# A planned instruction order: shared PSUM banks, a new price for changes of array use, and a seeded local search

## The chip, the cores and the metric

The kernel runs on one core of a Trainium2 chip. The metric is device time in microseconds (us) of one launch; lower is better. The engines are TensorE (PE, its weight loads are PEld), VectorE (DVE), ScalarE (ACT), GpSimd (POOL) and SyncE (SP), which issues nearly all DMAs. PSUM has eight banks of 512 float32 columns on 128 partitions; TensorE writes its products there, ScalarE and VectorE read them.

## The reference

Three blocks in a row, all in float32:

```python
# attention: q, k, v are (4, 12, 448, 64)
q_n, k_n = rmsnorm(q, g_q), rmsnorm(k, g_k)
attn = softmax(q_n @ k_n.T / 8)
x = (attn @ v), heads joined          # (4, 448, 768)
# gated block: d_ff = 1024
u, v = split(relu(x @ w_in))
v_s = w_spatial @ layernorm(v) + b_spatial
x = (u * v_s) @ w_out
# mixer: 448 -> 256 -> 448 over tokens, 768 -> 1536 -> 768 over channels
u = x + (relu(x.T @ w_tok1) @ w_tok2).T
out = u + relu(u @ w_ch1) @ w_ch2
```

## The kernel before, in words

**The work.** Attention runs over 24 pairs of heads (a slot each, method `slot` of class `Attention`). A slot loads q and k (`raw`), norms them, transposes them (`tp`), and for each of four groups of 112 queries makes the scores (`scores`, tiles `sc`, two banks a group), their negated row maxima (`nm`, VectorE), the exponentials (`e`, ScalarE), and the transposes of these (`turned`, tiles `tp`, copied out to `et`). From the ninth slot on (`HALVED = 8`) the transposes of a group go by halves of 64 and 48 rows into two banks opened together. `values` multiplies by v (tile `av`). Generators for the gated block (`moe`, products `vps`, `ups`, `sps`, `xps`; weights kept in DRAM as `wu_d`, `wo_d` and loaded as `wu`, `wo`) run beside attention for the batches that are done; the mixer follows: over tokens (`h1ps`, `u_ps`), then over channels (`up` with `h2ps`, `down` with `o_ps`), each by seven products in place of eight. Most products are made of three passes over numbers split into a high and a low part (`PASSES`). Copies of products out of PSUM have names of their own: `tg` for ups, `vr` for vps, `xo` for xps.

**The order.** The kernel does not issue its instructions where it names them. Class `Plan` records each as an `Op` with an engine, dependencies, a planned duration and a delay until others see the result (`estimate`, with fixed prices for each kind: on ScalarE 0.833 ns a column of the free size, 51 for an operand in PSUM, and 93 for each of a bias or scale tile and an accumulated output). At the end `issue` makes the order: `place` runs a list schedule on a planned clock, engine by engine. It takes the waiting instruction with the smallest weight (the most urgent), with these exceptions:

- TensorE: `op.parts` says how the array is used: 0 whole, 1 by halves of the rows, 2 by halves of the columns. An instruction with the same use as the last is preferred if its weight is within `NEAR` or `FAR` of the most urgent. A change of use adds `SWITCH` ns to the planned end.
- VectorE and GpSimd do not run at once where both are marked `port`.
- An instruction that opens PSUM tiles needs banks. `Banks` knows three kinds of tile, `sc` (scores, h1ps), `tp` (transposes) and `mm` (av, vps, ups, sps, xps, u_ps); the products of `up` and `down` rotate over the kinds. Each kind has a number of banks of its own in `OWN`. It may take a free bank only if what the other kinds still lack of their own stays free:

```python
spare = len(free_banks) - sum(max(0, n - held[x]) for x, n in Banks.OWN.items() if x != kind)
if spare < len(ks):
    blocked.append(i)
```

A bank comes free, on the planned clock, when its last reader is done; of the free ones the one that came free first is taken, and tiles of one kind open in the order of the program. Eight rounds alternate a forward placement with one backwards through the graph, whose times become the next weights (there the distances in `BACK` stand for the banks). The round with the shortest planned span gives the order in which all engines' instructions, DMAs on SyncE's queue among them, are written out. One line, 426, writes all instructions, so every row of the profile names L426 and the tiles tell the work apart.

The functions that the change touches:

Of the kernel before, what the change touches and what calls it, by code (L numbers as in the profile page):

```python
# [3 lines left out]

# [21 lines left out]
class Part:  # L26


    def __init__(self, tile_, shape, dtype, steps=(), box=None, dims=None):
        self.tile, self.shape, self.dtype, self.steps = tile_, tuple(shape), dtype, steps  # L30


        self.box = tuple((0, n) for n in self.shape) if box is None else box
        self.dims = tuple(range(len(self.shape))) if box is None else dims
# [94 lines left out]
class Banks:  # L129

    OWN = {"sc": 4, "tp": 2, "mm": 2}
    ALL = 8

    def __init__(self, pool):
        self.pool, self.tiles = pool, {kind: [] for kind in self.OWN}

# [11 lines left out]
class Plan:  # L150
# [112 lines left out]
    def hop(a, b):  # L263

        if a.engine == b.engine and not a.dma:
            return OWN[a.engine]
        return a.late + TO[b.engine]

    def place(self, before, after, lag, weight, tiles=None):
# [11 lines left out]
        if tiles is not None:  # L281
            opens, closes, users = tiles
            users = dict(users)
            free_banks = [(0.0, n) for n in range(Banks.ALL)]
            held = dict.fromkeys(Banks.OWN, 0)
            blocked = []
# [4 lines left out]
        while placed < len(ops):  # L291
# [35 lines left out]
            if tiles is not None and i in opens:  # L327
                ks = opens[i]
                kind = ks[0].psum
                spare = len(free_banks) - sum(max(0, n - held[x]) for x, n in Banks.OWN.items() if x != kind)  # L330
                if spare < len(ks):
# [53 lines left out]
    def issue(self, banks, rounds=8):  # L385

        ops = self.ops
        for op, users in self.later:
            op.deps.update(users)
        number = {op: i for i, op in enumerate(ops)}  # L390
        opens, closes, users, turns, rings = {}, {}, {}, [], []
        for kind, ring in banks.tiles.items():
            for n, t in enumerate(ring):
                us = list(dict.fromkeys(t.users))
                opens.setdefault(number[us[0]], []).append(t)
                users[t] = len(us)
                for u in us:
                    closes.setdefault(number[u], []).append(t)
                if n:
                    turns.append((ring[n - 1].users[0], us[0]))  # L400
                if n >= BACK[kind]:
                    rings.extend((u, us[0]) for u in ring[n - BACK[kind]].users)
        prev, succ, lag, _ = self.graph(turns)
        rprev, rsucc, _, back = self.graph(rings)
        weight = list(range(len(ops)))
        best = None
        for _ in range(rounds):
            start, span, bank = self.place(prev, succ, lag, weight, (opens, closes, users))
            if best is None or span < best[0]:
                best = (span, start, bank)  # L410
            late = [-(start[i] + op.cost) for i, op in enumerate(ops)]
            start, _, _ = self.place(rsucc, rprev, back, late)
            weight = [-(start[i] + op.cost) for i, op in enumerate(ops)]
        start = best[1]
        for t, n in best[2].items():
            t.bank = n
        for i in sorted(range(len(ops)), key=lambda i: (start[i], i)):
            op = ops[i]
            if op.engine == "fence":
                op.call()  # L420
                continue
            for x in (op, *op.more):
                fn, args, kwargs = x.call
                args = [a.real() if isinstance(a, Part) else a for a in args]
                kwargs = {k: a.real() if isinstance(a, Part) else a for k, a in kwargs.items()}
                getattr(getattr(self.nc, op.engine), fn)(*args, **kwargs)  # L426
# [3 lines left out]

SWITCH, NEAR, FAR, EARLY = 200, 2500, 10000, 95000
SHARED = {"vector": "gpsimd", "gpsimd": "vector"}


# [1 line left out]

OWN = {"tensor": 0, "scalar": 143, "vector": 127, "gpsimd": 100, "fence": 0}
TO = {"tensor": 100, "scalar": 0, "vector": 0, "gpsimd": 28, "sync": 0, "fence": 0}  # L440
# [1146 lines left out]
```

## Time and profile before

| | us |
|---|---|
| median of 3 runs | 865.27 |
| lowest, highest | 864.09, 868.58 |
| profiled execution, its own time | 869.1 |
| its span, first to last instruction | 867.3 |
| TensorE busy | 844.7 (97%) |
| VectorE busy | 687.4 (79%) |
| ScalarE busy | 532.5 (61%) |
| GpSimd busy | 416.0 (48%) |

The span is what the profiler sees between the program's first and last instruction; the time of a run also holds what lies around it. Matmuls are pipelined and their ends are modelled, so a share of 97% says that TensorE always had one under way, not that it ran at its best pace. For that one reads the starts of neighbouring pieces.

### The profile page before, as it was taken

Reading aid. Unit: us, or ns where it says so; the run is one execution under the profiler, and the core shown is the slowest. Engines: PE = TensorE matmul, PEld = TensorE weight load, DVE = VectorE, ACT = ScalarE, POOL = GpSimd, SP = SyncE. Lnnn points to the kernel's source line nnn. Section 1 sums busy time; section 2 is a strip of 40 time slices with the busy share of each in tenths; the row PEclk is TensorE's granted clock in tenths of the full one; section 3 lists DMA queues with packets and bytes.
Section 4 is the critical chain, followed back from the end, with each engine's and each line's share of the span. In section 5 each row is a group of like instructions: output and inputs, shape, how many; then the busy total and the mean of one; then the engine's idle time right before and its main releaser. Section 6 shows DMA issues by size and latency. Waiting matters only on the chain.

```text
span 867.3 us, 16458 instructions
## 1 busy us (share of the span) xinstructions
PE 844.7 (97%) x5544; PEld 707.0 (82%) x5544; DVE 687.4 (79%) x1343; ACT 532.5 (61%) x1278; POOL 416.0 (48%) x538
## 2 busy tenths in 40 slices
PE   6999999999999999999899999999999999999998
PEld 4544667777677787777789999999999999999998
DVE  5898899777887678876377577889989886999973
ACT  6999979778787768866253356655435654343331
POOL 3656646785676645566035223234433108425560
PEclk9999999999999999999999999999999999999999
DMA  6555765657636576453778678775765645751441
GB/s 167 148 145 160 193 193 149 199 131 240 185 94 155 144 224 189 107 156 94 245 253 246 209 227 265 246 247 187 206 165 144 204 126 171 237 155 56 146 155 65
DMA packets 153012, 152.34 MB, mean 176 GB/s; under 512 B 76896, under 2 KB 136096, under 8 KB 152928
## 3 DMA queue, kind: packets, MB, share of 16 engines
q1 hardware_dynamic: 152464, 151.26, 59.1%
q8 instruction: 44, 0.72, 0.3%
q14 instruction: 40, 0.33, 0.1%
q10 hardware_dynamic: 464, 0.03, 0.0%
HBM read 112.44 MB, written 38.80 MB: 174 GB/s over the span
## 4 chain that ended last, share of the span: by engine, by line
PE 74%; ACT 8%; DVE 6%; DMA 5%; POOL 3%; issue 2%; SPq 2%; ACTq 0%; POOLq 0%; DVEq 0%
PE h2ps L426 18%; PE o_ps L426 18%; PE xps L426 5%; PE ups L426 5%; PE tp L426 5%; PE av L426 5%; PE vps L426 4%; PE u_ps L426 4%; PE h1ps L426 4%; PE sps L426 3%; PE sc L426 3%; DMA wo<-wo_d 2%; ACT e L426 2%; SPq L426 2%; DMA raw<-in_k_dram 2%
## 5 line engine op out<-in xcount | busy, mean ns | idle before, releaser
L426 PE MATMUL h2ps<-op,w 128*128 128x448 f32 x756 | 154.2, 366 | 0.0
L426 PE MATMUL o_ps<-w,op 128*128 128x384 f32 x882 | 153.1, 334 | 0.0
L426 PEld LDWEIGHTS o_ps<-w,op 128*128 128x128 f32 x882 | 152.9, 188 | 0.0
L426 PEld LDWEIGHTS h2ps<-op,w 128*128 128x128 f32 x756 | 141.7, 188 | 11.1
L426 ACT ACTIVATE e<-sc,nm 112x448 f32<-112x448 f32 x184 | 118.6, 661 | 10.8 <-DVE nm L426 10.4
L426 DVE TENSOR_REDUCE nm<-sc 112x1 f32<-112x448 f32 x192 | 110.2, 613 | 11.3 <-PE sc L426 10.6
L426 POOL TENSOR_TENSOR src<-src 128x384 f32<-128x384 f32 x48 | 64.3, 1348 | 76.8 <-DMA src<-c_d 45.9
L426 ACT ACTIVATE op<-c 128x768 fp32r<-128x768 f32 x49 | 41.5, 847 | 80.6 <-PE o_ps L426 74.8
L426 POOL TENSOR_SCALAR e<-e,sums 112x448 f32<-112x448 f32 x112 | 72.3, 661 | 36.2 <-DVE sums L426 26.2
L426 PEld LDWEIGHTS tp<-ident,e 64*128 64x128 f32 (+2 forms) x1120 | 58.1, 139 | 33.4 <-issue 12.1
L426 ACT ACTIVATE et<-tp 128x448 f32<-128x448 f32 x144 | 70.5, 528 | 9.8 <-PE tp L426 9.4
L426 DVE TENSOR_SCALAR word<-word 128x256 f32<-128x256 f32 (+5 forms) x132 | 58.9, 450 | 20.6 <-ACT word L426 19.6
L426 DVE SCALAR_TENSOR_TENSOR word<-raw,word 128x256 uint32<-128x256 uint32 (+2 forms) x132 | 73.8, 561 | 1.6
L426 POOL TENSOR_TENSOR u<-u,o 128x384 f32<-128x384 f32 x28 | 41.1, 1483 | 67.6 <-ACT o L426 39.2
L426 PE MATMUL tp<-ident,e 48*128 48x48 f32 (+2 forms) x1120 | 69.3, 234 | 0.7 <-DVE et L426 0.4
L426 DVE TENSOR_TENSOR op<-c,op 128x768 fp32r<-128x768 f32 x49 | 58.7, 1198 | 10.2 <-ACT op L426 10.2
L426 PE MATMUL ups<-xp,wu 128*128 128x448 f32 x288 | 64.2, 369 | 0.0
L426 PE MATMUL av<-et,v 128*64 128x448 f32 x288 | 60.1, 548 | 2.7 <-ACT et L426 1.9
L426 PE MATMUL xps<-wo,g 128*128 128x384 f32 x288 | 57.0, 348 | 3.7 <-DMA wo<-wo_d 2.1
L426 PEld LDWEIGHTS ups<-xp,wu 128*128 128x128 f32 x288 | 53.4, 188 | 5.3 <-issue 0.3
L426 DVE TENSOR_TENSOR c<-c,h2ps 128x448 f32<-128x448 f32 x84 | 49.5, 613 | 10.1 <-PE h2ps L426 9.9
L426 PEld LDWEIGHTS xps<-wo,g 128*128 128x128 f32 x288 | 51.6, 193 | 5.7 <-DMA wo<-wo_d 2.1
(149 smaller groups left out, 1652.8 us busy)
## 6 DMA issues: line engine op xcount, KB each, us to landing
src<-c_d SPq DMA_DIRECT2D x132, 192.0 KB, 3.0
wu<-wu_d SPq DMA_DIRECT2D x16, 768.0 KB, 5.5
wo<-wo_d SPq DMA_DIRECT2D x16, 768.0 KB, 6.0
raw<-in_moe_w_ch_dram SPq DMA_DIRECT2D x36, 256.0 KB, 3.2
raw<-in_moe_w_ch_dram SPq DMA_DIRECT2D x24, 384.0 KB, 3.6
raw<-in_q_dram SPq DMA_DIRECT2D x48, 112.0 KB, 3.2
u<-u_d SPq DMA_DIRECT2D x28, 192.0 KB, 3.9
out_dram<-u SPq DMA_DIRECT2D x28, 192.0 KB, 2.0
```

The costliest lines, as they stand in the source:

```text
L426: getattr(getattr(self.nc, op.engine), fn)(*args, **kwargs)
```

## The change

Three edits, all in what makes the order. `OWN` leaves each kind fewer banks of its own, and three of the eight are shared. A change of array use costs 300 ns on the planned clock, where it was 200. And after the eight rounds come 250 steps of a local search with a fixed seed: each takes the weights of the best order so far, adds noise of 100, 300 or 1000 ns to those of the instructions whose planned start lies within 3 or 10 us of a point drawn from the first 460 us, places again, and keeps the order if its planned span is shorter. The search runs while the program is built.

```diff
--- before.py
+++ after.py
@@ -1,4 +1,5 @@
 import heapq
+import random
 import re
 from contextlib import ExitStack, contextmanager
 
@@ -130,7 +131,7 @@
 
 
 
-    OWN = {"sc": 4, "tp": 2, "mm": 2}
+    OWN = {"sc": 2, "tp": 2, "mm": 1}
     ALL = 8
 
     def __init__(self, pool):
@@ -407,10 +408,18 @@
         for _ in range(rounds):
             start, span, bank = self.place(prev, succ, lag, weight, (opens, closes, users))
             if best is None or span < best[0]:
-                best = (span, start, bank)
+                best = (span, start, bank, weight)
             late = [-(start[i] + op.cost) for i, op in enumerate(ops)]
             start, _, _ = self.place(rsucc, rprev, back, late)
             weight = [-(start[i] + op.cost) for i, op in enumerate(ops)]
+        rnd = random.Random(1)
+        for _ in range(250):
+            at, reach, size = rnd.uniform(0, TRIED), rnd.choice((3e3, 10e3)), rnd.choice((100, 300, 1000))
+            weight = [
+                w + rnd.gauss(0, size) if abs(s - at) < reach else w for s, w in zip(best[1], best[3])]
+            start, span, bank = self.place(prev, succ, lag, weight, (opens, closes, users))
+            if span < best[0]:
+                best = (span, start, bank, weight)
         start = best[1]
         for t, n in best[2].items():
             t.bank = n
@@ -430,7 +439,8 @@
 
 
 
-SWITCH, NEAR, FAR, EARLY = 200, 2500, 10000, 95000
+SWITCH, NEAR, FAR, EARLY = 300, 2500, 10000, 95000
+TRIED = 460e3
 SHARED = {"vector": "gpsimd", "gpsimd": "vector"}
```

## Rows read from the trace of the kernel before

**Rows 1.** By stretch: length, busy PE PEld DVE ACT POOL (xcount), clock, DMA, GB/s.
```profile
0.00:20.00 20.00, 12.41 (x67) 8.98 (x68) 11.03 (x30) 12.09 (x30) 5.09 (x21) 0.91 0.69 166
20.00:95.00 75.00, 70.40 (x437) 36.91 (x434) 67.40 (x148) 73.51 (x208) 47.94 (x72) 1.00 0.58 152
95.00:450.00 355.00, 348.14 (x2778) 262.64 (x2777) 272.23 (x661) 258.69 (x710) 209.06 (x330) 1.00 0.61 176
450.00:867.00 417.00, 413.76 (x2270) 398.45 (x2268) 336.79 (x508) 188.18 (x333) 153.88 (x116) 1.00 0.59 180
```

**Rows 2.** Chain that ended last, in order: start us, us, what.
```profile
429.17 15.19 PE vps L426 x66
...
560.87 149.98 PE h2ps L426 x740
710.85 152.92 PE o_ps L426 x882
```

**Rows 3.** Groups of TensorE, 95 to 450 us: count | busy us, mean ns | idle before.
```profile
L426 PE MATMUL vps<-wv,xp 128*128 128x512 f32 x216 | 55.4, 402 | 0.0
L426 PE MATMUL ups<-xp,wu 128*128 128x448 f32 x234 | 52.6, 370 | 0.0
L426 PE MATMUL sc<-kt,qt 64*112 64x448 f32 x384 | 49.5, 377 | 1.1 <-ACT e L426 0.4 <-DVE et L426 0.3 <-ACT tg L426 0.3
L426 PE MATMUL av<-et,v 128*64 128x448 f32 x224 | 46.3, 548 | 1.2 <-DVE et L426 0.7 <-ACT et L426 0.4
L426 PE MATMUL xps<-wo,g 128*128 128x384 f32 x216 | 43.4, 352 | 3.7 <-DMA wo<-wo_d 2.1 <-ACT g L426 0.7 <-POOL g L426 0.6
L426 PE MATMUL tp<-ident,e 64*128 64x64 f32 x448 | 40.5, 227 | 0.0
L426 PE MATMUL tp<-ident,e 48*128 48x48 f32 x448 | 39.3, 225 | 0.7 <-DVE et L426 0.4 <-ACT et L426 0.4
L426 PE MATMUL sps<-ws,vn 128*128 128x448 f32 x138 | 31.9, 372 | 0.1
L426 PE MATMUL av<-et,vrest 128*64 128x448 f32 x76 | 17.5, 539 | 0.0
```

**Rows 4.** TensorE in order of time, 329 to 365 us: start us, us, what.
```profile
329.82 1.90 PE L426 MATMUL vps<-wv,xp 128*128 128x512 f32 x7
331.65 0.65 PE L426 MATMUL tp<-ident,e 64*128 64x64 f32 x14
332.23 1.20 PE L426 MATMUL vps<-wv,xp 128*128 128x512 f32 x4
333.35 0.65 PE L426 MATMUL tp<-ident,raw 64*128 64x64 f32 x14
...
363.15 0.65 PE L426 MATMUL tp<-ident,e 64*128 64x64 f32 x14
363.61 1.44 PE L426 MATMUL sc<-kt,qt 64*112 64x448 f32 x12
364.89 0.59 PE L426 MATMUL tp<-ident,e 48*128 48x48 f32 x14
```

**Rows 5.** TensorE in order of time: first and last of 115 changes, a wait between.
```profile
95.17 1.72 PE L426 MATMUL av<-et,v 128*64 128x448 f32 x8
...
419.33 5.31 PE L426 MATMUL xps<-wo,g 128*128 128x384 f32 x20 [1.80 <-DMA wo<-wo_d]
...
425.94 2.48 PE L426 MATMUL av<-et,v 128*64 128x448 f32 x12 [0.73 <-DVE et L426]
...
429.10 12.54 PE L426 MATMUL vps<-wv,xp 128*128 128x512 f32 x54
```

**Rows 6.** Groups of ScalarE, 95 to 450 us.
```profile
L426 ACT ACTIVATE e<-sc,nm 112x448 f32<-112x448 f32 x139 | 88.0, 644 | 10.7 <-DVE nm L426 10.4
...
L426 ACT ACTIVATE tg<-ups 128x448 f32<-128x448 f32 x13 | 7.0, 542 | 5.9 <-PE ups L426 5.9
```

**Rows 7.** Busy time by stretch, behind the wait at 419 us.
```profile
420.00:425.00 5.00, 5.00 (x32) 4.75 (x30) 2.79 (x8) 1.66 (x5) 0.00 (x0) 0.66 0.70 236
```

## The prediction

> **What bounds the kernel now.** I read the busy time by stretch first [rows 1]. The profiled execution took 869.1 us, of which 867 are the span; TensorE is busy for 844.7 of these (12.4 + 70.4 + 348.1 + 413.8). By that alone 22.3 us could be won, and the rows show where they lie. From 450 us on, TensorE lacks only 3.2 us of 417, the tail behind the last product. From 95 to 450 us it lacks 6.9 us of 355. From 20 to 95 us it lacks 4.6 us of 75, but there ScalarE is busy for 73.5 of the 75: TensorE waits for an engine that is itself full. The other 7.6 us lie in the first 20 us, where the first loads and norms set the pace.
>
> A busy TensorE need not be at its pace, so I read next the chain that ended last, which has long unbroken pieces of one kind of product [rows 2]. They give paces: 15.19/66 = 230.2 ns for 512 columns, 149.98/740 = 202.7 ns for 448, 152.92/882 = 173.4 ns for 384. The last two pieces run without a pause from 561 to 864 us: there the order has nothing to give. With these paces I count the stretch from 95 to 450 us by its groups [rows 3]: 216 vps products x 0.2302 = 49.7 us, 372 ups and sps products x 0.2027 = 75.4, 216 xps x 0.1734 = 37.5. For the narrow uses of the array the paces come from the order of time [rows 4, 5]: 12 score products between 363.61 and 364.89, 0.107 us each, so 384 x 0.107 = 41.1; 14 short transposes between 363.15 and 363.61, 0.033 each, so 896 x 0.033 = 29.6; 16 value products between 425.94 and 429.10, which with 0.12 for the change behind them (below) are 0.190 each, so 300 x 0.190 = 57.0. That is 290.3 us. The nine smaller groups of that view, 394 instructions, are an estimate of 34 us by the same paces. So 355 - 6.9 - 324.3 = 23.8 us of busy time are not work at pace.
>
> Most of it is what a change of array use costs. The array is used whole, by halves of its rows (scores, short transposes) or by halves of its columns (values). In the trace there are 115 changes between 95 and 450 us, from the one into the value products at 95.17 to the one out of them at 429.10 [rows 5], 65 before that and none later. The short visits in [rows 4] price one: 7 vps products from 329.82 to 331.65 take 1.83 us where 7 x 0.2302 = 1.61 are due, and 4 from 332.23 to 333.35 take 1.12 where 0.92 are due, so entering costs 0.21; the 14 transposes between them hold until 332.23, 0.58 us against 0.46, so leaving costs 0.12. That is 0.17 each; the count gives 23.8/115 = 0.21. I take 0.18. The planner's old price of 200 ns is near it, the new one of 300 is too high.
>
> **The change part by part.** No instruction is added or removed on the device; the search runs while the program is built. All terms are therefore terms of order, in the first 450 us. The search shifts urgencies of instructions that start up to 460 us, and some microseconds beyond; what comes later stands at pace. I cost the late part at nothing: other engines' work moved there lies beside TensorE's products, and if that cover were gone it would cost its own length.
>
> *The shared banks.* The transposes of a halved probability tile need two tp banks together. With two in all, a second such group must wait until both are copied out, which takes ScalarE about what the copy of a whole-array product takes, 0.542 us [rows 6]. With 2 + 3 possible, two groups can stand open, and scores can still reach five. So one visit to the half-row use can hold more. *The price* does not enter the rule that picks the next instruction; it enters the planned clock, and through it which candidate is shortest. *The search* keeps one of 250 variants only where the planned span is shorter, so waits and changes are both pressed down on the planner's clock.
>
> How much, the trace cannot show; I bound it. Those around the 19 value visits among the 115 changes must stay. 41 visits start from the whole array. If none is merged, 0 us is won; if each third is, 13 visits less with two changes and often a third, 38 changes x 0.18 = 6.8 us. Visits with only one group of 14 transposes, like the two of [rows 4], are the ones that can merge; I take 10 visits, 20 changes, **-3.6 us**.
>
> Waits from 95 to 450 us are 6.9 us. Upper end: all go, -6.9. Lower end: one late load more like that of the matrix wo, for which the xps products at 419.33 stood 1.80 us [rows 5]. I take somewhat under half, **-3.0 us**, since part of them follows from durations that the planner has too short: it prices an exponential at 610 ns (0.833 x 448 + 51 + 2 x 93), and the trace has 644 [rows 6], so a plan without gaps on paper has some on the chip.
>
> After that wait of 1.80 us the granted clock was 0.66 of full between 420 and 425 us [rows 7]: 2.4 GHz for a part, 1.2 for the rest. The 20 xps products took 5.31 us instead of 20 x 0.1734 = 3.47, 1.8 us lost. If that load comes in time, this comes back too; another may take its place. Half of it, **-0.9 us**.
>
> From 20 to 95 us there are 63 changes, but ScalarE has only 1.5 us to spare [rows 1]. Fewer changes there would only make TensorE wait longer for ScalarE. I take 0, with -1.5 (ScalarE full throughout) and +1.5 as ends. The DMAs keep their number and sizes; SyncE's queue is reordered with the rest, and a load that comes to stand behind others is the lower end named above.
>
> Sum: -3.6 - 3.0 - 0.9 = **-7.5 us**, so 869.1 - 7.5 = 861.6 us for the profiled execution. The median of the runs before is 865.27, 3.8 us below the profiled execution; by the same ratio the forecast is 865.27 x 861.6/869.1 = 857.8, **858 us**. The ends add up to -6.8 - 6.9 - 1.8 - 1.5 = -17 and to 1.80 + 1.8 (a late load with its clock) + 1.5 = +5 us.
>
> What a measurement tells from no change is about 0.5%, 4.3 us, so the limits are 861 and 869.6 us.
>
> **The rivals.** *Gain on paper only.* Every shorter plan is chosen on the planner's clock, and the shortest of 250 is also the one that leans most on its too short durations. The waits that go return elsewhere; only some five merged visits stay: 10 x 0.18 = 1.8 us, 863.5 us. For it: the 34 ns by which each of 139 exponentials in this stretch is mispriced sum to 4.7 us of ScalarE. Against it: ScalarE is busy there for only 259 of 355 us. The case that the search finds hardly anything over a start that is itself new, made with other banks and another price, ends here too.
>
> *More than forecast.* A third of the visits merge, most waits and the slow clock go: -6.8 - 5.0 - 1.8 = -13.6 us, 852 us. For it: the search works on every stretch again and again. Against it: the banks were only one of the reasons for a short visit; what it needs must also be ready.
>
> *Slower: one assured bank for the whole-array products.* These had two banks of their own and now have one, if scores and transposes hold the shared three. Then each of some 70 groups from 95 to 450 us (216 vps, 234 ups and 216 xps in 18s, 138 sps in 11s, 300 values in 16s) waits for the copy of the one before, 0.542 us [rows 6] and its issue, say 0.6. All would be 42 us. It decides from (7.5 + 4.3)/0.6 = 20 groups on; with half of them it is +21 - 7.5 = +13.5, about 879 us. For it: scores may now grow to five banks. Against it: the planner sees the bank return before it places a group, and TensorE has other work to place meanwhile, as the 6.9 us of waits in 355 show.
>
> *Slower: the clock.* Each stretch at 1.2 GHz like that after 419 us is, with its wait, 1.80 + 1.8 = 3.6 us; four of them beyond the gain give 14.4 - 7.5 = +6.9, 872 us; it decides from (7.5 + 4.3)/3.6, just over three. Against it: with eight banks in rotation throughout, the clock from 20 to 867 us is 1.00 in each long stretch, so one short fall in all [rows 1, 7]. The Trainium skill, TensorE: Matmul & The Clock Gate, section "A second HAM failure mode: psum-queue depth-cycling", says that a kernel which cycles through its banks can idle so often between groups that the clock swings; by it, more cycling through shared banks would bring this rival about. No row here shows more than the one fall, and that behind a DMA.
>
> **How the numbers follow.** Forecast, -4.3 to -11 us, 854 to 861: 0.50. More: 0.13. Paper only: 0.24. One bank: 0.08. Clock and late loads: 0.05. So faster 0.63, same 0.24, slower 0.13. The range leaves out the slower rivals and the farthest part of the paper case, some 0.16, and the end of the larger gain beyond 851, some 0.04: 851 to 866.
>
> **What would show it.** Right: the stretch of h2ps and o_ps products as long as now; fewer than 100 changes of array use in the middle stage, fewer visits of 14 transposes alone; TensorE's waits there under 4 us; the long h2ps piece beginning some 7 us before 561. Wrong: as many changes and waits as now, under other names; waits of whole-array products for ScalarE's copies (tg, vr, xo); a granted clock under 1 in several stretches. ScalarE no longer full before 95 us, with TensorE further along, would mean that the early stage gave what I left at 0. The forecast also falls if the late stage has gaps, since it is counted at nothing.

## The result, and the profile after

The changed kernel takes 858.8 us (median of 4 runs, 857.19 to 859.86); the kernel before, on the same chip, 866.63. The ratio is 0.9916, 95% interval 0.9897 to 0.9934: 7.3 us less, where 7.5 were forecast. The profiled execution took 859.86 us, its span is 857.7 us. All instructions are now written out by line 435.

Busy time by stretch of the changed kernel, columns as in [rows 1]:

```profile
0.00:20.00 20.00, 13.59 (x72) 11.21 (x73) 11.93 (x32) 12.38 (x31) 6.30 (x22) 0.94 0.70 166
20.00:95.00 75.00, 68.88 (x418) 38.78 (x418) 63.21 (x140) 70.48 (x198) 47.26 (x71) 0.95 0.56 155
95.00:450.00 355.00, 352.18 (x2835) 266.66 (x2836) 276.12 (x677) 264.27 (x726) 207.05 (x332) 1.00 0.61 180
450.00:857.00 407.00, 403.70 (x2225) 390.34 (x2223) 324.86 (x497) 184.43 (x325) 145.73 (x114) 1.00 0.59 181
```

From 95 to 450 us TensorE now lacks 2.8 us where it lacked 6.9, and runs 57 instructions more in the same time. From 20 to 95 us it lacks 6.1 us where it lacked 4.6, at a granted clock of 0.95, and runs 19 instructions fewer; by 95 us it has started 13 fewer than before. So the early stage lost, and the middle stage won more than the whole gain. What TensorE waited for from 95 to 450 us, in total, times, longest:

```profile
PE tp L435 <- DVE xp L435: 0.8, 1, 0.8
PE xps L435 <- ACT e L435: 0.7, 1, 0.7
PE sc L435 <- DVE et L435: 0.5, 1, 0.5
PE tp L435 <- ACT whole L435: 0.4, 1, 0.4
PE sps L435 <- POOL vn L435: 0.4, 1, 0.4
```

The late load of wo, 2.1 us in [rows 3], is no longer among them. TensorE in order of time: the first change of array use from 95 us on (at 95.77), a visit, and the last change.

```profile
94.83 1.01 PE L435 MATMUL sc<-whole 64*112 64x448 f32 x4
95.77 1.72 PE L435 MATMUL av<-et,v 128*64 128x448 f32 x8
...
271.52 1.52 PE L435 MATMUL tp<-ident,e 64*128 64x64 f32 x42
272.86 1.45 PE L435 MATMUL sc<-kt,qt 64*112 64x448 f32 x12
274.14 0.59 PE L435 MATMUL tp<-ident,raw 64*128 64x64 f32 x14
274.67 2.48 PE L435 MATMUL av<-et,v 128*64 128x448 f32 x12
...
419.90 5.28 PE L435 MATMUL vps<-wv,xp 128*128 128x512 f32 x22
```

42 transposes stand in a row, three groups of a halved probability tile, and with scores and the transposes of the next slot they make one visit. There are 149 changes of array use in all (180 before), 100 in the middle stage (115). Visits that hold nothing but one group of 14 transposes, 19 in the middle stage before, are 2. The last is at 419.90 us, 9.2 us earlier than in [rows 5]. From there on nothing changed: from the first o_ps product to the last it is 701.2 to 853.9 us, 152.7 us in both kernels.

The loss lies here, TensorE from 83 to 91 us in order of time, and the busy time by stretch from 80 to 86 and from 86 to 93 us:

```profile
83.84 0.32 PE L435 MATMUL tp<-ident,e 112*128 112x112 f32 x1 [1.35 <-ACT e L435]
...
86.94 3.33 PE L435 MATMUL sc<-whole 64*112 64x448 f32 x8 [1.88 <-ACT whole L435]
90.21 0.45 PE L435 MATMUL tp<-ident,wide 112*128 112x112 f32 x1
```

```profile
80.00:86.00 6.00, 3.60 (x26) 2.31 (x26) 6.00 (x14) 5.17 (x14) 2.35 (x3) 1.00 0.50 134
86.00:93.00 7.00, 6.05 (x24) 3.87 (x25) 4.03 (x11) 4.68 (x15) 5.68 (x10) 0.51 0.60 167
```

TensorE waits 1.35 and 1.88 us for ScalarE, and from 86 us on, when the second wait is still under way, the granted clock is 0.51: 1.2 GHz for nearly all of these 7 us. Eight score products take 3.3 us; the four at 94.83 us take 0.94, so eight would take 1.9 at 2.4 GHz. ScalarE itself had stood shortly before, 1.59 us, for a row maximum (`nm`) that VectorE made only after work on weights, the longest piece of it 1.5 us (`word`); VectorE is busy for all 6 us from 80 to 86:

```profile
77.54 1.53 DVE L435 SCALAR_TENSOR_TENSOR word<-raw,word 128x512 uint32<-128x512 uint32 x1
80.00 0.62 DVE L435 TENSOR_REDUCE nm<-sc 112x1 f32<-112x448 f32 x1
80.66 0.64 ACT L435 ACTIVATE e<-sc,nm 112x448 f32<-112x448 f32 x1 [1.59 <-DVE nm L435]
```

### The profile page after: what moved, and what is told of

It is laid out like the page before. It is cut to its first block, busy times and chain, and to the rows that moved or that the text cites. A ratio compares the mean times of both kernels' runs of the same rounds, so it can differ in the third digit from the quotient of the medians.

```text
span 857.7 us, 16446 instructions
## 1 busy us (share of the span) xinstructions
PE 838.4 (98%) x5544; PEld 707.0 (82%) x5544; DVE 676.1 (79%) x1343; ACT 531.6 (62%) x1278; POOL 406.3 (47%) x538
## 4 chain that ended last, share of the span: by engine, by line
PE 80%; ACT 8%; DVE 5%; DMA 3%; issue 1%; POOL 1%; SPq 1%; ACTq 0%; POOLq 0%; DVEq 0%
PE o_ps L435 18%; PE h2ps L435 18%; PE ups L435 6%; PE av L435 6%; PE xps L435 6%; PE vps L435 6%; PE tp L435 5%; PE sc L435 5%; PE sps L435 4%; PE u_ps L435 4%; PE h1ps L435 4%; ACT e L435 3%; DMA raw<-in_moe_w_in_dram 2%; ACT et L435 2%; DVE wpart L435 1%
## 5 line engine op out<-in xcount | busy, mean ns | idle before, releaser
L435 POOL TENSOR_TENSOR src<-src 128x384 f32<-128x384 f32 x48 | 60.2, 1261 | 75.3 <-DMA src<-c_d 47.5
L435 ACT ACTIVATE et<-tp 128x448 f32<-128x448 f32 (+1 forms) x144 | 66.9, 527 | 18.6 <-PE tp L435 18.5
L435 DVE SCALAR_TENSOR_TENSOR word<-raw,word 128x256 uint32<-128x256 uint32 (+2 forms) x132 | 71.0, 541 | 1.5
L435 PE MATMUL tp<-ident,e 48*128 48x48 f32 (+2 forms) x1120 | 65.7, 235 | 2.6 <-ACT e L435 1.3
L435 DVE TENSOR_SCALAR word<-word 128x256 f32<-128x256 f32 (+5 forms) x132 | 55.4, 424 | 13.8 <-ACT word L435 13.0
L435 DVE TENSOR_TENSOR op<-c,op 128x768 fp32r<-128x768 f32 x49 | 55.9, 1140 | 10.2 <-ACT op L435 10.2
L435 PE MATMUL vps<-wv,xp 128*128 128x512 f32 x216 | 54.8, 401 | 0.0
L435 PE MATMUL xps<-wo,g 128*128 128x384 f32 x288 | 53.8, 339 | 0.7 <-ACT e L435 0.7
```

## The experiments

Theory A: the shared banks give the gain, since they let visits merge. Theory B: the search gives it. Theory C: the price does. All times below are medians; each ratio is against the kernel before on the same chip, which took 866.8 to 867.5 us there. Changes of array use and TensorE's waits (stretch less busy time) are read from each run's trace, so from one execution, while executions of one kernel differ by several us: the profiled one of the search alone took 865.9 us, the longest of its ten, that of the old division until 95 us 863.7, the shortest of its ten.

| kernel | us | ratio, 95% interval | changes, all | waits 20 to 95 | waits 95 to 450 |
|---|---|---|---|---|---|
| before | 866.6 | 1 | 180 | 4.6 | 6.9 |
| the change | 858.8 | 0.9916, 0.9897 to 0.9934 | 149 | 6.1 | 2.8 |
| banks alone | 864.3 | 0.9976, 0.9961 to 0.9991 | 153 | 5.2 | 4.7 |
| search alone | 862.1 | 0.9952, 0.9934 to 0.9969 | 183 | 3.9 | 5.6 |
| banks, price | 864.2 | 0.9971, 0.9958 to 0.9984 | 144 | 7.3 | 4.0 |
| banks, search | 861.4 | 0.9948, 0.9931 to 0.9965 | 149 | 5.0 | 2.8 |
| the change, seed 2 | 860.8 | 0.9938, 0.9911 to 0.9966 | 141 | 7.3 | 1.5 |
| the change, seed 5 | 862.0 | 0.9946, 0.9927 to 0.9965 | 139 | 6.2 | 3.5 |
| price 500 | 876.9 | 1.0116, 1.0101 to 1.0131 | 133 | 7.7 | 9.0 |
| price 1000 | 919.3 | 1.0617, 1.0571 to 1.0663 | 106 | 11.2 | 35.6 |
| transposes held to two banks | 869.4 | 1.0019, 0.9996 to 1.0042 | 171 | 2.9 | 7.8 |
| only transposes beyond the old share | 862.8 | 0.9949, 0.9933 to 0.9965 | 152 | 4.0 | 3.4 |
| old division until 95 us | 867.1 | 0.9991, 0.9972 to 1.0011 | 160 | 4.3 | 4.3 |

**The parts one by one.** The banks alone (search and price taken out of the change):

```diff
-    OWN = {"sc": 4, "tp": 2, "mm": 2}
+    OWN = {"sc": 2, "tp": 2, "mm": 1}
```

> The changed banks alone (2, 2 and 1 of their own, three shared), the old price of 200 ns and no search. Theory A, the shared banks merge visits of TensorE to its half-row use: most of the gain is here, some 30 changes of array use fewer in all than 180, at about 0.2 us each 6 us, so 859 to 862 us. Theory B, the search is what shortens the order: no gain, 864 to 868 us. Theory C, the price: no gain here either.

The search alone, with the old banks and 200 ns:

> The 250 steps alone, with the old banks (4, 2, 2) and the old price. Theory A: changes of array use stay at about 180, waits shrink a little, 864 to 867 us. Theory B: most of the gain, 858 to 861 us, with the middle stage's waits under 4 us. Theory C: no gain, 864 to 868 us.

The change without its search:

```diff
-        for _ in range(250):
+        for _ in range(0):
```

> The change without its search: shared banks and the price of 300 ns. Theory A: 858 to 862 us, within 3 us of the whole change. Theory B: 864 us or more. Theory C, the price picks the order with fewer changes: 2 us or more below the kernel with the banks alone.

The change with the old price:

```diff
-SWITCH, NEAR, FAR, EARLY = 300, 2500, 10000, 95000
+SWITCH, NEAR, FAR, EARLY = 200, 2500, 10000, 95000
```

> The change with the old price: shared banks and the search at 200 ns. Theory A and theory B: within 2 us of the whole change, 857 to 861 us. Theory C, the price matters: 862 us or more, with more changes of array use than the whole change has (149).

None of the three theories holds. B's limits came nearest: both kernels without the search stayed within them (864.3 and 864.2 us), and the search alone missed its limit by 1.1 us. The banks do what A says to the visits: 27 changes fewer without any search. But of the 5 to 6 us that these are worth only 2.1 arrive. The search alone leaves the changes as they are (183) and takes 1.2 us off the waits from 95 to 450 us; it gives 4.2 us, more than A and less than B expected. Busy time by stretch, the kernel with the banks alone and the one with the search alone:

```profile
20.00:95.00 75.00, 69.82 (x434) 40.38 (x436) 67.20 (x148) 72.45 (x205) 49.25 (x69) 0.98 0.56 150
95.00:450.00 355.00, 350.33 (x2814) 263.91 (x2813) 279.58 (x667) 262.46 (x720) 208.53 (x332) 1.00 0.62 178
```

```profile
20.00:95.00 75.00, 71.09 (x436) 36.69 (x436) 67.45 (x149) 73.77 (x209) 47.67 (x72) 0.98 0.59 156
95.00:450.00 355.00, 349.36 (x2786) 264.16 (x2783) 272.59 (x664) 261.13 (x711) 206.71 (x331) 0.99 0.61 174
```

With the banks, TensorE runs 36 instructions more than before in the middle stage; in the early one it is busy for 0.6 us less. With the search, the early stage is the better one and the middle stage stays near [rows 1], with a clock that falls twice (0.99). Together with the price they gain 3 us more than the better of the two alone. At the old price, on the same chip, banks and search together give 4.5 us, only 0.3 more than the search alone, although 34 changes and 2.9 us of waits in the middle stage are gone. So how much of a merged visit arrives as time is not shown by these runs. The price by itself does nothing that can be told (0.9976 and 0.9971 without search); with the search, 0.9948 against 0.9916 could be the price or the draw.

**The draw.** The same change with another seed:

```diff
-        rnd = random.Random(1)
+        rnd = random.Random(2)
```

> The whole change with another seed of the search, nothing else: its order has 141 changes of array use where the change has 149. If what the search adds to the banks and the price is a real pressing down of waits and changes, any seed gives it: 857 to 860.5 us. If the change's 858.8 us are a lucky draw among orders that scatter by 2 to 3 us, this one lies nearer to the kernel without the search: 861 to 864 us.

> A third seed; 139 changes of array use. As for the second: 857 to 860.5 us if the search works by itself, 861 to 864 us if it was the draw. Both seeds on one side settle it.

Neither seed reached the range that I had set for a search that works by itself: seed 2 (860.8 us) lies just between the two ranges, seed 5 (862.0 us) in that of a lucky draw. Still, all three seeds (0.9916, 0.9938, 0.9946) lie below the kernel without the search (0.9971). The intervals of seeds 2 and 5 overlap with its interval, so that the search itself is worth some 2 to 5 us is likely, not shown by each. The change's own seed is the best of the three, by 1.9 and 2.6 us; seed 5, with ten changes fewer, is slower. So some 2 us of the 7.3 may be luck of the draw, and the price of 300 ns, which differs from the old one by about as much as the seeds do among themselves, stays open.

**What the banks are for.** Transposes held to two banks at once, all else as in the change:

```diff
-                if spare < len(ks):
+                if spare < len(ks) or kind == "tp" and held[kind] + len(ks) > 2:
```

> The whole change, but transposes may never hold more than two banks at once; scores and whole-array products share the rest as in the change. Its order has 171 changes of array use, the change 149. If it is the second pair of banks for transposes that lets visits merge, 22 changes come back at 0.2 us each: 862 to 865 us. If scores or products are what profits from the shared banks, it stays at 857 to 860 us.

The whole gain is gone, more than expected: the changes come back to 171, the visits of 14 transposes alone to 15, the waits to 7.8 us.

```profile
20.00:95.00 75.00, 72.13 (x429) 39.29 (x427) 66.74 (x142) 71.39 (x202) 42.84 (x69) 0.97 0.55 148
95.00:450.00 355.00, 347.19 (x2785) 260.32 (x2786) 269.90 (x670) 261.88 (x718) 208.55 (x331) 1.00 0.63 177
```

The middle stage is that of [rows 1] again, with 2785 instructions for 2778. The search alone had only two transpose banks as well and kept 4.2 us, so the cap explains the visits, but not all of the 9 us between this run and the change: the sharing of the other two kinds, the price and the draw of this one order are in them too. The counterpart, in which only transposes can go beyond their old share:

```diff
-                if spare < len(ks):
+                if spare < len(ks) or kind == "sc" and held[kind] + len(ks) > 4 or kind == "mm" and held[kind] + len(ks) > 2:
```

> The counterpart of the run with transposes held to two banks: the whole change, but scores may hold at most four banks and whole-array products at most two, as before, so that only transposes can reach beyond their old share. The order has 152 changes of array use, near the change's 149. If the second pair of transpose banks is the whole effect of the sharing, 857 to 861 us, as the change itself (858.8). If scores or whole-array products need more banks as well, the gain is lost in part: 862 to 866 us, with more waits from 95 to 450 us than the change's 2.8 us.

Busy time by stretch:

```profile
20.00:95.00 75.00, 71.01 (x441) 39.53 (x441) 63.07 (x143) 72.71 (x204) 47.01 (x69) 0.98 0.52 140
95.00:450.00 355.00, 351.58 (x2816) 265.01 (x2813) 271.84 (x680) 263.43 (x725) 213.41 (x334) 1.00 0.61 180
```

It has the visits (152 changes) and a middle stage near the change's (3.4 us of waits), but 0.9949: 4.4 us, some 60% of the gain, within the second of the ranges that I had set. So further banks for transposes are what makes visits merge: 152 changes with them, 171 without them. In time, however, this run equals the search alone (0.9952 with 183 changes). What the sharing of scores and whole-array products is worth stays open: between this run and the change lie 3 us of gain, between the search alone and the run with the cap 6 us of loss, each time by one order, and in the second case with the price changed too.

**The early stage.** The old division until 95 us of the planned clock, shared banks after:

```diff
-                spare = len(free_banks) - sum(max(0, n - held[x]) for x, n in Banks.OWN.items() if x != kind)
+                own = {"sc": 4, "tp": 2, "mm": 2} if t < EARLY else Banks.OWN
+                spare = len(free_banks) - sum(max(0, n - held[x]) for x, n in own.items() if x != kind)
```

> The whole change, but until 95 us of the planned clock the banks are divided as before (4, 2, 2), and shared after that. In the changed kernel the first vps products start at 103.7 us, 3.9 us later than before, with more waits from 20 to 95 us (6.1 against 4.6 us) and a fall of the clock at 86 us. If the shared banks are what loses time in the early stage, the first vps products come at 100 us or sooner and the run takes 855 to 858 us. If the late start is a matter of that one order and no loss of the banks, 859 to 863 us; its order has 160 changes, 11 more.

My theory fell. The first vps products start at 103.4 us, as late as in the change (103.7), and the run is no faster than before, 4 us above the higher of the two ranges. In the run with only transposes beyond their share they start at 99.7. First vps products of the change, of this run and of that one:

```profile
103.66 1.89 PE L435 MATMUL vps<-wv,xp 128*128 128x512 f32 x7
103.43 0.96 PE L436 MATMUL vps<-wv,xp 128*128 128x512 f32 x3
99.73 0.50 PE L435 MATMUL vps<-wv,xp 128*128 128x512 f32 x1 [0.20 <-ACT e L435]
```

So shared banks do not force the late start. But in the other orders with all three kinds shared, at prices up to 500 ns, these products start between 102 and 106 us, with the old banks at 98.7 and 99.8; its cause stays open. So does the lost gain of this run: the profiled execution (863.7 us) has 20 changes and 3 us of waits less than the kernel before, but the median of the ten is 3.4 us longer.

**A higher price.** 500 and 1000 ns in place of 300:

> The whole change with 500 ns for a change of array use in place of 300; its order has 133 changes, 16 fewer. If fewer changes are what counts, at 0.2 us each, 3 us less: 854 to 857 us. If the early stage, where ScalarE is full, gives fewer changes back as waits, as between 20 and 95 us in the changed kernel (16 fewer changes there, and more waits and a fall of the clock), 858 to 862 us.

> The same with 1000 ns; its order has 106 changes, 43 fewer than the change. If fewer changes count, up to 8.6 us less: 850 to 854 us. If they come back as waits, the sum of TensorE's waits in the first 450 us is over 20 us (now 15.4) and the time is 858 us or more.

The orders have 133 and 106 changes, and both kernels are slower than before, the first by 10 us, outside both of its ranges, the second by 53 us. At 500 ns the waits of the first 450 us are 24.5 us where the change has 15.4; that is 9 of the 17.5 us between the two profiled spans (875.2 and 857.7), and the rest is not assigned. Waits of TensorE until its last change of array use, and busy time by stretch, at 1000 ns:

```profile
PE tp L435 <- POOL e L435: 8.4, 13, 4.3
PE tp L435 <- POOL wide L435: 8.0, 5, 4.4
PE sc L435 <- ACT et L435: 6.5, 5, 1.8
PE tp L435 <- ACT et L435: 4.6, 3, 2.0
```

```profile
20.00:95.00 75.00, 63.77 (x370) 39.29 (x371) 61.05 (x132) 67.66 (x187) 42.53 (x68) 0.91 0.60 160
95.00:450.00 355.00, 319.37 (x2490) 232.39 (x2489) 257.37 (x614) 245.25 (x676) 191.33 (x311) 0.95 0.52 147
```

TensorE lacks 35.6 us in the middle stage, and its clock is 0.95 of full there, at 1.2 GHz for about a tenth of the time. The waits are the links of attention's own chain: normalised exponentials (`e`), copies of transposes (`et`). I read it so: on the planned clock a change that costs 1000 ns is also 800 ns in which other engines get ready, and the planner fills the rest of their latency with work; on the chip those 800 ns don't exist and TensorE stands. That reading was argued from the waits, not tried by itself.

**The cost of a change, by itself.** In the late stage, where TensorE has no waits, each group of h2ps products gets one short half-row product behind it, each group of o_ps products one short whole-array product; nothing reads them, and the planner does not know of the 168 changes. `run_and` stands in place of `run` for both kinds of group:

```diff
+    def run_and(ps, ops, left, right):
+
+        for _ in run(ps, ops, 100):
+            pass
+        last = nc.ops[-1]
+        no = psum.tile([P, 512], "tp", "visit")
+        nc.joined = [last]
+        nc.tensor.matmul(no[:, :64], left, right, start=True, stop=True)
+        nc.joined = None
```

> What a change of array use costs, measured by itself in the late stage, where TensorE has no waits. Behind each of the 84 groups of nine h2ps products stands one more product of 64 rows and 64 columns, whose result nothing reads: 168 changes more that the planner does not know of. Behind each of the 49 groups of o_ps products stands one of the same 64 columns that uses the array whole: no change. At 0.17 to 0.21 us a change, the stage from the first h2ps to the first o_ps product grows from 154.4 to between 185 and 192 us; if changes are hidden between long products, to less than 172; if 300 ns were right, to over 205. The o_ps stage grows by 49 short products, some 2 to 3 us.

The products of the two stages: durations in ns (least, median, most), first and last start, first in the change, then with the short products.

```profile
L435 PE MATMUL h2ps<-op,w x756: 358/365/448, 546.8 to 701.0; 128*128 128x448 f32 x189
...
L435 PE MATMUL o_ps<-w,op x882: 333/334/346, 701.2 to 853.9; 128*128 128x384 f32 x177
```

```profile
L435 PE MATMUL h2ps<-op,w x756: 358/368/473, 546.5 to 738.6; 128*128 128x448 f32 x189
...
L435 PE MATMUL o_ps<-w,op x882: 334/334/443, 739.1 to 897.4; 128*128 128x384 f32 x177
```

From the first h2ps to the first o_ps product it was 154.4 us and is 192.6: 38.2 us for 84 visits, 0.455 us each. The o_ps stage grew from 152.7 to 158.3, 5.6 us for 49 products, 0.114 us each without a change. The first stage is just above the 185 to 192 us that I expected, the growth of the second twice the 2 to 3 us; both come from the one execution of this kernel. If a half-row product costs no more than a whole-array one, a change costs between (0.455 - 0.114)/2 = 0.17 and 0.455/2 = 0.23 us.

## Why the prediction was right, and where it was not

The time came out, and so did most signs: nothing after the last change of array use moved, TensorE's waits in the middle stage are under 4 us, visits of 14 transposes alone are 2 where they were 19, and the gain lies between 95 and 420 us but for 1.2 us of the first 20. The changes there are 100, where fewer than 100 were to show it. That 7.5 meets 7.3 so closely is in part luck: the middle stage gave more than forecast, the early one took some back, and the two other seeds give 5.4 and 4.7 us. The terms, by the profiled executions (span 867.3 to 857.7, -9.6 us):

- **Changes in the middle stage**, forecast 20 fewer at 0.18 us, -3.6. Measured: 15 fewer, -2.6 to -3.5 at the price now measured (0.17 to 0.23; the short visits of [rows 4] gave its lower end). The mechanism was the one described, longer visits by further open groups of transposes: held to two banks, the order has 171 changes instead of 149.
- **Waits in the middle stage**, forecast -3.0, measured -4.0 (6.9 to 2.8).
- **The clock in the middle stage**, forecast -0.9 as half of 1.8; the fall behind the late load is gone, -1.8.
- **The early stage**, forecast 0 with ends of 1.5 us either way. This step failed: 16 changes fewer (63 to 47), worth -2.7 to -3.7, but 1.5 us more waits and 7 us at 1.2 GHz, for 6.05 of which TensorE was busy, some 3 us lost. That makes +0.8 to +1.8, and ScalarE, which I took for full throughout, is busy for 70.5 us where it was for 73.5; it stood for VectorE's row maxima, 2.5 us in three waits. Nor were all of the 4.6 us of waits before waits for ScalarE: 1.9 of them were for GpSimd, in these rows of the kernel before, 20 to 95 us:

```profile
PE tp L426 <- POOL raw L426: 1.5, 3, 0.9
PE av L426 <- ACT et L426: 1.4, 3, 0.6
PE sc L426 <- ACT whole L426: 0.7, 2, 0.5
PE tp L426 <- POOL wide L426: 0.4, 1, 0.4
```

What is lost there differs by order: with seed 2 the granted clock from 20 to 95 us is 0.99, with seed 5 0.93, the change has 0.95.

- **The first 20 us** gave 1.2 us, which I had not forecast. These terms make -7.8 to -9.7 where 9.6 were measured.

**A price that I had wrong.** I held that the planner prices an exponential too short, 610 ns against 644 [rows 6], and built a part of the waits' term and of the rival "gain on paper" on it. In the changed kernel's chain that ended last, there are two exponentials with the reads of their accumulated sums, that follow each other without a pause:

```profile
94.14 1.23 ACT e L435 x4
```

That is 0.615 us for one with its read. The 644 ns are a duration that reaches into the next instruction; the planner's 610 is right. So the 4.7 us of ScalarE that were to speak for that rival do not exist.

**The rivals.** One assured bank for the whole-array products did not show: no wait of vps, ups or xps for copies of their kind is among the rows above; the 0.7 us for which xps waited for an exponential may be one for a shared bank. The clock rival showed in the early stage, once, with waits of 1.35 and 1.88 us. The Trainium skill, TensorE: Matmul & The Clock Gate, section "A second HAM failure mode: psum-queue depth-cycling", was cited for it; the middle stage with shared banks shows 1.00 with 2.8 us of waits in 355, so the trace of this change shows no such swing there, and the fall in the early stage came with waits for ScalarE. That only paper would gain is refuted by the change itself, whose waits in the middle stage fell on the chip too, and by the search alone, 0.9952 (0.9934 to 0.9969).

**What I did not separate** in the prediction is which part works. It had the banks merge visits and the search press down changes and waits both. The runs say: the banks take the changes away, the search alone takes waits away but no changes, neither gives more than 4.2 us alone, and the price is not to be told from the seed. How the 7.3 us divide among the three edits and the draw stays open.

## What to carry to other kernels

Where an order is planned, look first for the resource that forces short visits to an expensive mode of an engine; here shared banks, above all further ones for one kind of tile, did for the visits what a search over urgencies alone did not (153 changes against 183). But do not take fewer visits for time before it is measured: alone, those banks gave 2.1 us and the search 4.2. Run a seeded search with more than one seed before its last 2 us are believed. A price in a planner should not be raised far above what the chip takes in order to discourage something: 300 ns for a change that costs about 200 could not be told from 200, but at 500 and 1000 ns the kernel became slower, with more waits. As I read it, time that exists only on the planned clock is used there as cover for other engines.

## What was not expected of the hardware

A lone whole-array product of 64 columns between products of 384 cost 0.114 us, where 384 columns take 0.173; by the paces of [rows 2] (0.1734 for 384, 0.2302 for 512) 64 columns would be about 0.03. Whether its own weight load sets this was not tried. And waits of under 2 us, twice within 4.5 us, went with 7 us at 1.2 GHz in the change; in the kernel with the price of 1000 ns such falls are spread over the first 450 us (granted clock 0.91 and 0.95), so that its waits cost more than they last. Part of the scatter between executions of one kernel goes with the clock: of the ten of the banks alone, the four at a mean granted clock of 0.996 or 0.997 took 861.6 to 863.3 us, the six at 0.990 to 0.994 864.1 to 865.7.
